# X from strided columns of transposed q, and output rows in token order (linear attention followed by a sentence-level mixture of experts, one core)

## Chip, core and metric

One NeuronCore of a Trainium2 chip runs the kernel; the other cores are idle. The metric is the device time of one execution in microseconds. Three runs of the kernel before took 342.43, 341.39 and 339.92 us, median 341.39.

## What is computed

Eight sentences (batch b) of 576 tokens, eight heads of 64 columns. Linear attention: q gets a softmax over its 64 columns, k a softmax over the tokens, then a 64 x 64 matrix per head is multiplied with q. The result x (576 x 512 for a sentence) goes through one expert of eight, chosen for the whole sentence from the mean of x over its tokens.

```
q_s = softmax(q over d);  k_s = softmax(k over tokens)
kv  = einsum('bhsd,bhse->bhde', k_s, v)
x   = einsum('bhsd,bhde->bhse', q_s, kv)          # then heads side by side: (8, 576, 512)
logits = x.mean(axis=1) @ w_gate;  e = argmax(logits);  gate = softmax(logits)[e]
out[b] = gate * (relu(x[b] @ w1[e]) @ w2[e])      # w1[e]: 512 x 1024, w2[e]: 1024 x 512
```

## The kernel before

**Tokens.** An input tile holds two heads on the 64-partition halves and two in the free dimension; partition p has the nine tokens 9p to 9p + 8 side by side (`pair_src`, L91, with J = 9). So token 9p + j is row p of block j. The transposes of q (L150) are made block by block: column 64j + p of `qt` is token 9p + j. All that follows keeps this blocked order of tokens: x (`xt`), the hidden layer h (`hsb`) and the rows of the output.

**Attention of one sentence** (`attention`, L110) is a generator in steps. Exponentials of q and k on ScalarE (L118, L123), v to fp16 on GpSimd (L129), the sums and the scaling of q on VectorE (L134, L137). For each of two halves i: 18 transposes on TensorE (L150) and two copies to `qt` on VectorE (L157); 18 matmuls k x v (L164); the 128 x 128 `kv` on VectorE (L173). Then for each of two g one chunk c = 2i + g of x: a matmul of 512 columns (L182) and one of 64 (L183), evacuated by VectorE to `xt`, which also adds up the columns for the mean (L184, L188). So a sentence has four chunks. Then the gate's logits (L196), argmax, and the expert's weights by DMAs that GpSimd issues (L211, L216, L217); they are cast from fp32 to fp16 on the way.

**Expert of one sentence** (`moe`, L235 on). Eight blocks of 128 hidden columns: four matmuls of 512 tokens (L243) and four of 64 (L248) each, and a Relu, on ScalarE for even blocks (L253), on VectorE for odd ones (L255); one Relu for all the 64-token tails (L257). Then five output blocks of 128 tokens (64 in the last): eight matmuls (L264), a scaling copy to `osb` on ScalarE (L269), and a store that SyncE issues (L271). `osb` has four buffers. In blocked order rows 128 st to 128 st + 127 are the tokens 9p + 2 st and 9p + 2 st + 1 for all 64 p, so the destination is

```
out_j = out.rearrange("b (p j) d -> b j p d", j=J)        # L96
nc.sync.dma_start(out=out_j[b, js], in_=osb[0:rows])      # L271: 2 x 64 rows of 2 KB, 1 x 64 in the last
```

**Order.** TensorE runs in the order in which the program is written: attention 0 and 1 first; then for each b the steps of the expert of sentence b, with one step of attention b + 2 after each. For sentences 6 and 7 there is no attention beside the expert. The other engines' orders are set by the scheduler of the language; each engine takes its instructions in order. SyncE issues the inputs of six sentences, then the five stores of sentence 0, the inputs of the seventh sentence, the stores of sentence 1, the inputs of the eighth, and then only stores.

Of the kernel before, what the change touches and what calls it, by code (L numbers as in the profile page):

```python
# [19 lines left out]
def kernel(  # L20
# [12 lines left out]
    nc = tc.nc  # L33

    B, H, S, Dh = q.shape
    D, E = moe_w_gate.shape
    F = moe_w1.shape[2]
    J = S // 64
    SM = 512
    ST = S - SM  # L40
    NF = F // 128
    ND = D // 128

# [24 lines left out]
    ones_f32 = consts.tile([128, 1], FP32)  # L68
# [22 lines left out]
    def pair_src(t, b, i):  # L91

        return t[b].rearrange("(i n g) (p j) d -> i (g p) n (j d)", i=2, n=2, p=64)[i]


    out_j = out.rearrange("b (p j) d -> b j p d", j=J)  # L96

    state = {}
    nv = [0]
# [10 lines left out]
    def attention(b, tiles, roomy):  # L110
        xt = xt_pool.tile([128, ND, S], FP16, name="xt")
        pooled = gat_pool.tile([128, ND], FP32, name="pooled")
        x_tag, x_bufs = ("po", 2) if roomy else ("x", 1)
        t_tag = "hm" if roomy else "tk"
        eqs, eks, vas = [], [], []
        for i in range(2):
            eq = e_pool.tile([128, J, 2, Dh], FP16, name="eq")
            nc.scalar.activation(  # L118
                out=eq.rearrange("p j n d -> p n j d"),
                in_=tiles["q", i].rearrange("p n (j d) -> p n j d", j=J), func=AF.Exp,  # L120
            )
            ek = e_pool.tile([128, J, 2, Dh], FP16, name="ek")
            nc.scalar.activation(  # L123
                out=ek.rearrange("p j n d -> p n j d"),
                in_=tiles["k", i].rearrange("p n (j d) -> p n j d", j=J), func=AF.Exp,
            )
            va = v_aug[nv[0] % NVB]
            nv[0] += 1
            nc.gpsimd.tensor_copy(  # L129
                out=va[:, :, 1:].rearrange("p j (n d) -> p n j d", n=2),  # L130
                in_=tiles["v", i].rearrange("p n (j d) -> p n j d", j=J),
            )
            qs = stat.tile([128, J, 2], FP32, name="qs")
            nc.vector.tensor_reduce(out=qs, in_=eq, op=ALU.add, axis=AX.X)  # L134
            qsi = stat.tile([128, J, 2], FP32, name="qsi")
            nc.vector.reciprocal(out=qsi, in_=qs)
            nc.vector.tensor_tensor(  # L137
                out=eq, in0=eq, in1=qsi.unsqueeze(3).to_broadcast([128, J, 2, Dh]), op=ALU.mult,
            )
            eqs.append(eq)  # L140
            eks.append(ek)
            vas.append(va)
        yield
        for i in range(2):
            eq, ek, va = eqs[i], eks[i], vas[i]
            tps = [bank(t_tag, 2) for g in range(2)]
            for j in range(J):
                for g in range(2):
                    r = slice(64 * g, 64 * g + 64)
                    nc.tensor.transpose(  # L150
                        out=tps[g].bitcast(FP16)[:, 64 * j:64 * j + 64],
                        in_=eq[r, j], identity=ident[r, r],
                    )
            qts = []
            for g in range(2):
                qt = qt_pool.tile([128, S], FP16, name="qt")
                nc.vector.tensor_copy(out=qt, in_=tps[g].bitcast(FP16)[:, 0:S])  # L157
                qts.append(qt)
            yield
            kps = [bank("tk", 2) for g in range(2)]  # L160
            for j in range(J):
                for g in range(2):
                    r = slice(64 * g, 64 * g + 64)
                    nc.tensor.matmul(  # L164
                        kps[g][:, 0:129], lhsT=ek[r, j], rhs=va[r, j],
                        start=(j == 0), stop=(j == J - 1),
                    )
            kvs = []
            for g in range(2):
                icv = kv_pool.tile([128, 1], FP32, name="icv")  # L170
                nc.vector.reciprocal(out=icv, in_=kps[g][:, 0:1])
                kv = kv_pool.tile([128, 128], FP16, name="kv")
                nc.vector.scalar_tensor_tensor(  # L173
                    out=kv, in0=kps[g][:, 1:129], scalar=icv, in1=blkmask, op0=ALU.mult, op1=ALU.mult,
                )
                kvs.append(kv)
            yield
            for g in range(2):
                c = 2 * i + g
                px = bank(x_tag, x_bufs)  # L180
                pxt = kps[g][:, 192:256]
                nc.tensor.matmul(px, lhsT=kvs[g], rhs=qts[g][:, 0:SM], start=True, stop=True)  # L182
                nc.tensor.matmul(pxt, lhsT=kvs[g], rhs=qts[g][:, SM:S], start=True, stop=True)  # L183
                nc.vector.tensor_tensor_reduce(  # L184
                    out=xt[:, c, 0:SM], in0=px, in1=ones_f32.to_broadcast([128, SM]),
                    scale=1.0, scalar=0.0, op0=ALU.mult, op1=ALU.add, accum_out=pooled[:, c:c + 1],
                )
                nc.vector.tensor_tensor_reduce(  # L188
                    out=xt[:, c, SM:S], in0=pxt, in1=ones_f32.to_broadcast([128, ST]),
                    scale=1.0, scalar=pooled[:, c:c + 1], op0=ALU.mult, op1=ALU.add,  # L190
                    accum_out=pooled[:, c:c + 1],
                )
                yield
        pg = bank(x_tag, x_bufs)
        for c in range(ND):
            nc.tensor.matmul(  # L196
                pg[0:1, 0:E], lhsT=pooled[:, c:c + 1], rhs=wg_sb[:, c, :],
                start=(c == 0), stop=(c == ND - 1),
            )
        zz = gat_pool.tile([1, E], FP32, name="zz")  # L200
        nc.vector.tensor_copy(out=zz, in_=pg[0:1, 0:E])
        mx8 = gat_pool.tile([1, 8], FP32, name="mx8")
        nc.vector.max(out=mx8, in_=zz)
        eidx = gat_pool.tile([1, 8], U32, name="eidx")
        nc.vector.max_index(out=eidx, in_max=mx8, in_values=zz)
        e_val = nc.values_load(eidx[0:1, 0:1], engines=[ET.Pool], min_val=0, max_val=E - 1)
        w1_sb = w_pool.tile([128, ND, F], FP16, name="w1_sb")
        w1_src = moe_w1[ds(e_val, 1)].rearrange("o (i h g e) f -> i h e (o g) f", i=2, h=2, g=2)
        for i in range(2):
            for h in range(2):  # L210
                nc.gpsimd.dma_start(  # L211
                    out=w1_sb[64 * h:64 * h + 64, 2 * i:2 * i + 2, :], in_=w1_src[i, h]
                )
        w2_sb = w_pool.tile([128, NF, D], FP16, name="w2_sb")
        w2_src = moe_w2[ds(e_val, 1)].rearrange("o (c p) n -> p (o c) n", p=128)
        nc.gpsimd.dma_start(out=w2_sb[:, 0:4], in_=w2_src[:, 0:4])  # L216
        nc.gpsimd.dma_start(out=w2_sb[:, 4:8], in_=w2_src[:, 4:8])  # L217

        nmx = gat_pool.tile([1, 1], FP32, name="nmx")
        nc.vector.tensor_single_scalar(out=nmx, in_=mx8[:, 0:1], scalar=-1.0, op=ALU.mult)  # L220
        ex = gat_pool.tile([1, E], FP32, name="ex")
        sm = gat_pool.tile([1, 1], FP32, name="sm")
        nc.scalar.activation(out=ex, in_=zz, func=AF.Exp, bias=nmx, accum_out=sm)
        gt = gat_pool.tile([1, 1], FP32, name="gt")
        nc.vector.reciprocal(out=gt, in_=sm)  # L225
        state[b] = [xt, gt, w1_sb, w2_sb]
        yield
        pg2 = bank(x_tag, x_bufs)
        nc.tensor.matmul(pg2[:, 0:1], lhsT=ones_row, rhs=gt, start=True, stop=True)
        gate = gat_pool.tile([128, 1], FP32, name="gate")  # L230
        nc.vector.tensor_copy(out=gate, in_=pg2[:, 0:1])
        state[b][1] = gate
        yield

    def moe(b):  # L235
        xt, gate, w1_sb, w2_sb = state.pop(b)
# [23 lines left out]
        for st in range(5):  # L260
            rows = 128 if st < 4 else ST
            po = bank("po", 2)
            for fc in range(NF):
                nc.tensor.matmul(  # L264
                    po[0:rows], lhsT=hsb[:, fc, st * 128:st * 128 + rows], rhs=w2_sb[:, fc, :],
                    start=(fc == 0), stop=(fc == NF - 1),
                )
            osb = o_pool.tile([128, D], FP32, name="osb")
            nc.scalar.mul(osb[0:rows], po[0:rows], gate[0:rows])  # L269
            js = slice(2 * st, min(2 * st + 2, J))  # L270
            nc.sync.dma_start(out=out_j[b, js], in_=osb[0:rows])  # L271
            yield

    def drain(gen):
# [51 lines left out]
```

## Time and profile before

| what | value |
|---|---|
| median of 3 runs | 341.39 us |
| profiled execution | 341.65 us |
| its span (first to last instruction) | 340.0 us |
| mean granted TensorE clock | 0.85 |
| TensorE busy | 193.5 us (57%) |
| VectorE busy | 123.6 us (36%) |
| ScalarE busy | 89.6 us (26%) |
| GpSimd busy | 52.1 us (15%) |
| DMA queue of SyncE (inputs, stores) | 17856 packets, 37.75 MB, 31.4% of 16 engines |
| DMA queue of GpSimd (weights) | 13056 packets, 16.78 MB, 29.3% of 16 engines |

No engine is busy for more than 57% of the span, and the two DMA queues together take 61% of the sixteen DMA engines. Busy time is an average over stages, so it does not say what is waited for; the chain of work that ended last, the waits and the timelines do. DMA share is the mean over the core's 16 DMA engines: one engine working all the time is 1/16 = 0.06. It can come out over 1 where packets overlap on an engine. Stretches are given in us from the start of the span.

### The profile page before, as it was taken

To read this page: it belongs to the slowest core of one execution; us is meant where nothing else is said; L and a number is where in the kernel's file an instruction comes from. 1 tells how busy PE (TensorE), PEld (TensorE's weight loads), DVE (VectorE), ACT (ScalarE), POOL (GpSimd) and SP (SyncE) were. 2 spreads that over 40 slices of the span, in tenths; PEclk is the share of its full clock that TensorE was granted. 3 is DMA by queue.
4 is the path that set the end of the run, shared out by engine and by line. 5 is a ranking of instruction groups with operands and counts; after the bars stand their busy time and mean duration, and the time that the engine had idled before them with its cause. 6 is when DMAs were issued, how large, how long until landed. Compare 5 with 4: busy or idle time off the path is not lost.

```text
span 340.0 us, 4144 instructions
## 1 busy us (share of the span) xinstructions
PE 193.5 (57%) x1552; PEld 95.5 (28%) x1552; DVE 123.6 (36%) x365; ACT 89.6 (26%) x130; POOL 52.1 (15%) x73
## 2 busy tenths in 40 slices
PE   0344387880068930889107895960769885479400
PEld 0223144440024420344103443530335341134100
DVE  3699949510058110780106816710236020011000
ACT  2644235210044300442004434210123230123100
POOL 1325261330001410014100141040000400000000
PEclk9999999995559985699755999996779998599955
DMA  7999999999619791199811149179121781112111
GB/s 262 396 391 378 278 294 280 290 284 285 139 65 332 197 187 36 58 338 223 149 36 64 41 80 196 43 140 166 37 67 52 140 150 38 65 51 66 51 64 42
DMA packets 31508, 54.81 MB, mean 161 GB/s; under 512 B 2304, under 2 KB 10496, under 8 KB 31488
## 3 DMA queue, kind: packets, MB, share of 16 engines
q1 hardware_dynamic: 17856, 37.75, 31.4%
q0 software_dynamic: 13056, 16.78, 29.3%
q8 instruction: 12, 0.20, 0.2%
q10 hardware_dynamic: 576, 0.02, 0.1%
q14 instruction: 8, 0.07, 0.1%
HBM read 61.88 MB, written 9.44 MB: 210 GB/s over the span
## 4 chain that ended last, share of the span: by engine, by line
DMA 48%; DVE 19%; PE 18%; ACT 5%; issue 2%; SPq 1%; ACTq 1%; POOL 0%; DVEq 0%; POOLq 0%
DMA out_dram<-osb 45%; PE hm L243 8%; DVE qs L134 5%; PE po L264 5%; DVE eq L137 4%; DVE xt L184 3%; ACT osb L269 2%; DMA wg_sb<-in_moe_w_gate_dram 2%; DVE hsb L255 2%; ACT eq L118 2%; PE x L182 1%; DMA v_in<-in_v_dram 1%; DVE kv L173 1%; SPq L271 1%; ACT hsb L253 1%
## 5 line engine op out<-in xcount | busy, mean ns | idle before, releaser
L243 PE MATMUL hm<-xt,w_sb 128*128 128x512 f16 x256 | 74.5, 421 | 60.9 <-ACT hsb L253 60.9
L264 PE MATMUL po<-w_sb,hsb 128*128 128x512 f16 (+1 forms) x320 | 77.8, 393 | 22.9 <-ACT osb L269 22.9
L269 ACT ACTIVATE osb<-po,gate 128x512 f32<-128x512 f32 (+1 forms) x40 | 27.2, 686 | 151.6 <-DMA out_dram<-osb 120.8
L264 PEld LDWEIGHTS <-hsb 128*128 128x128 f16 (+1 forms) x320 | 31.0, 103 | 61.0 <-issue 31.3
L243 PEld LDWEIGHTS <-w_sb 128*128 128x128 f16 x256 | 22.5, 105 | 88.0 <-issue 72.6
L134 DVE TENSOR_REDUCE qs<-eq 128x18 f32<-128x1152 f16 x16 | 21.5, 1345 | 64.9 <-ACT eq L118 64.9
L129 POOL CAST va<-v_in 128x1152 f16<-128x1152 f32 x16 | 19.7, 1239 | 132.7 <-PE tk L164 82.2
L255 DVE TENSOR_SCALAR hsb<-hm 128x512 f16<-128x512 f32 x32 | 22.1, 690 | 44.6 <-PE hm L243 44.0
L211 POOL DMA_DIRECT2D w_sb<-in_moe_w_dram x32 | 19.3, 623 | 81.6 <-DVE gt L225 39.6
L253 ACT ACTIVATE hsb<-hm 128x512 f16<-128x512 f32 x32 | 18.8, 588 | 41.8 <-PE hm L243 41.8
L157 DVE COPY qt<-tk 128x576 f16<-128x576 f16 x24 | 9.9, 453 | 52.7 <-PE tk L150 52.7
L248 PEld LDWEIGHTS <-w_sb 128*128 128x128 f16 x256 | 17.7, 104 | 18.1 <-issue 5.4
L137 DVE TENSOR_TENSOR eq<-eq,qsi 128x1152 f16<-128x1152 f16 x16 | 21.8, 1360 | 0.1
L118 ACT ACTIVATE eq<-q_in 128x1152 f16<-128x1152 f32 x16 | 18.6, 1160 | 9.8 <-DMA q_in<-in_q_dram 5.7
L123 ACT ACTIVATE ek<-k_in 128x1152 f16<-128x1152 f32 x16 | 18.5, 1157 | 7.5 <-PE tk L164 4.2
L248 PE MATMUL ht<-xt,w_sb 128*128 128x64 f16 x256 | 19.2, 200 | 0.0
L184 DVE CUSTOM_DVE_ANT_0 xt<-x,ones_f 128x512 f16<-128x512 f32 x24 | 16.4, 684 | 6.6 <-PE tk L183 6.6
L182 PE MATMUL x<-qt,kv 128*128 128x512 f16 x24 | 10.8, 449 | 11.6 <-DVE kv L173 7.0
L164 PE MATMUL tk<-va,ek 64*128 64x129 f16 x288 | 13.8, 246 | 2.9 <-DVE pooled L188 1.9
L164 PEld LDWEIGHTS <-ek 64*128 64x128 f16 x288 | 10.5, 108 | 4.1 <-issue 2.1
L150 PEld LDWEIGHTS <-eq 64*128 64x128 f16 x288 | 6.4, 103 | 12.6 <-issue 11.8
L182 PE MATMUL po<-qt,kv 128*128 128x512 f16 x8 | 4.4, 612 | 9.3 <-DVE kv L173 9.3
(49 smaller groups left out, 106.1 us busy)
## 6 DMA issues: line engine op xcount, KB each, us to landing
q_in<-in_q_dram SPq DMA_DIRECT2D x16, 576.0 KB
k_in<-in_k_dram SPq DMA_DIRECT2D x16, 576.0 KB
v_in<-in_v_dram SPq DMA_DIRECT2D x16, 576.0 KB
w_sb<-in_moe_w_dram POOLq DMA_DIRECT2D x32, 256.0 KB, 10.6
w_sb<-in_moe_w_dram POOLq DMA_DIRECT2D x16, 512.0 KB, 20.7
out_dram<-osb SPq DMA_DIRECT2D x32, 256.0 KB
out_dram<-osb SPq DMA_DIRECT2D x8, 128.0 KB
wg_sb<-in_moe_w_gate_dram ACTq DMA_DIRECT2D x4, 4.0 KB
```

Of the source, the lines that this page charges most:

```text
L118: nc.scalar.activation(out=eq.rearrange("p j n d -> p n j d"), in_=tiles["q", i].rearrange("p n (j d) -> p n j d", j=J), func=AF.Exp,)
L129: nc.gpsimd.tensor_copy(out=va[:, :, 1:].rearrange("p j (n d) -> p n j d", n=2), in_=tiles["v", i].rearrange("p n (j d) -> p n j d", j=J),)
L134: nc.vector.tensor_reduce(out=qs, in_=eq, op=ALU.add, axis=AX.X)
L137: nc.vector.tensor_tensor(out=eq, in0=eq, in1=qsi.unsqueeze(3).to_broadcast([128, J, 2, Dh]), op=ALU.mult,)
L164: nc.tensor.matmul(kps[g][:, 0:129], lhsT=ek[r, j], rhs=va[r, j], start=(j == 0), stop=(j == J - 1),)
L184: nc.vector.tensor_tensor_reduce(out=xt[:, c, 0:SM], in0=px, in1=ones_f32.to_broadcast([128, SM]), scale=1.0, scalar=0.0, op0=ALU.mult, op ...
L243: nc.tensor.matmul(phm, lhsT=w1_sb[:, c, fsl], rhs=xt[:, c, 0:SM], start=(c == 0), stop=(c == ND - 1),)
L248: nc.tensor.matmul(pht[:, fc * ST:(fc + 1) * ST], lhsT=w1_sb[:, c, fsl], rhs=xt[:, c, SM:S], start=(fc == 0 and c == 0), stop=(fc == NF - ...
L253: nc.scalar.activation(out=hsb[:, fc, 0:SM], in_=phm, func=AF.Relu)
L255: nc.vector.tensor_single_scalar(out=hsb[:, fc, 0:SM], in_=phm, scalar=0.0, op=ALU.max)
L264: nc.tensor.matmul(po[0:rows], lhsT=hsb[:, fc, st * 128:st * 128 + rows], rhs=w2_sb[:, fc, :], start=(fc == 0), stop=(fc == NF - 1),)
L269: nc.scalar.mul(osb[0:rows], po[0:rows], gate[0:rows])
```

## The change

The X matmul reads the columns of `qt` in the order of tokens. `qn` is `qt` seen as (p, j): nine columns 64 apart, then the next p. The first matmul takes p from 0 to 55 (56 x 9 = 504 tokens), the second the remaining 8 x 9 = 72; before it was 512 and 64. So `xt`, `hsb` and the output rows are in the natural order of tokens, and rows 128 st to 128 st + 127 of the output are one contiguous block, to which the store writes. The expert's code is otherwise the same, with its 512 and 64 tokens.

```diff
--- before.py
+++ after.py
@@ -38,6 +38,7 @@
     J = S // 64
     SM = 512
     ST = S - SM
+    XM = 56 * J
     NF = F // 128
     ND = D // 128
 
@@ -91,9 +92,6 @@
     def pair_src(t, b, i):
 
         return t[b].rearrange("(i n g) (p j) d -> i (g p) n (j d)", i=2, n=2, p=64)[i]
-
-
-    out_j = out.rearrange("b (p j) d -> b j p d", j=J)
 
     state = {}
     nv = [0]
@@ -178,15 +176,16 @@
             for g in range(2):
                 c = 2 * i + g
                 px = bank(x_tag, x_bufs)
-                pxt = kps[g][:, 192:256]
-                nc.tensor.matmul(px, lhsT=kvs[g], rhs=qts[g][:, 0:SM], start=True, stop=True)
-                nc.tensor.matmul(pxt, lhsT=kvs[g], rhs=qts[g][:, SM:S], start=True, stop=True)
+                pxt = kps[g][:, 192:192 + S - XM]
+                qn = qts[g].rearrange("q (j p) -> q p j", j=J)
+                nc.tensor.matmul(px[:, 0:XM], lhsT=kvs[g], rhs=qn[:, 0:56], start=True, stop=True)
+                nc.tensor.matmul(pxt, lhsT=kvs[g], rhs=qn[:, 56:64], start=True, stop=True)
                 nc.vector.tensor_tensor_reduce(
-                    out=xt[:, c, 0:SM], in0=px, in1=ones_f32.to_broadcast([128, SM]),
+                    out=xt[:, c, 0:XM], in0=px[:, 0:XM], in1=ones_f32.to_broadcast([128, XM]),
                     scale=1.0, scalar=0.0, op0=ALU.mult, op1=ALU.add, accum_out=pooled[:, c:c + 1],
                 )
                 nc.vector.tensor_tensor_reduce(
-                    out=xt[:, c, SM:S], in0=pxt, in1=ones_f32.to_broadcast([128, ST]),
+                    out=xt[:, c, XM:S], in0=pxt, in1=ones_f32.to_broadcast([128, S - XM]),
                     scale=1.0, scalar=pooled[:, c:c + 1], op0=ALU.mult, op1=ALU.add,
                     accum_out=pooled[:, c:c + 1],
                 )
@@ -267,8 +266,7 @@
                 )
             osb = o_pool.tile([128, D], FP32, name="osb")
             nc.scalar.mul(osb[0:rows], po[0:rows], gate[0:rows])
-            js = slice(2 * st, min(2 * st + 2, J))
-            nc.sync.dma_start(out=out_j[b, js], in_=osb[0:rows])
+            nc.sync.dma_start(out=out[b, st * 128:st * 128 + rows, :], in_=osb[0:rows])
             yield
 
     def drain(gen):
```

Every engine has the same instructions in the same order as before; what differs is widths and shapes. On SyncE's queue, at the end of the first six sentences' inputs and the stores of sentence 0, before:

```order
L106 DMA k_in<-in_k_dram 128x2x576
L106 DMA v_in<-in_v_dram 128x2x576
L271 DMA out_dram<-osb 2x64x512 x4
L271 DMA out_dram<-osb 64x512
L106 DMA q_in<-in_q_dram 128x2x576
```

and there with the change (its lines count two less):

```order
L104 DMA k_in<-in_k_dram 128x2x576
L104 DMA v_in<-in_v_dram 128x2x576
L269 DMA out_dram<-osb 128x512 x4
L269 DMA out_dram<-osb 64x512
L104 DMA q_in<-in_q_dram 128x2x576
```

Nothing moved; the four stores of 128 rows have lost the outer dimension of two, and the last one, of 64 rows, is as it was.

## Rows read from the trace of the kernel before

**Rows 1.** The page's part 4, the chain that ended last.

```profile
DMA 48%; DVE 19%; PE 18%; ACT 5%; issue 2%; SPq 1%; ACTq 1%; POOL 0%; DVEq 0%; POOLq 0%
DMA out_dram<-osb 45%; PE hm L243 8%; DVE qs L134 5%; PE po L264 5%; DVE eq L137 4%; DVE xt L184 3%; ACT osb L269 2%; DMA wg_sb<-in_moe_w_gate_dram 2%; DVE hsb L255 2%; ACT eq L118 2%; PE x L182 1%; DMA v_in<-in_v_dram 1%; DVE kv L173 1%; S
```

**Rows 2.** Waits: engine line <- waited for: us in total, times, longest us.

```profile
ACT osb L269 <- DMA out_dram<-osb: 120.8, 14, 23.8
```

**Rows 3.** ScalarE's timeline: start us, us, engine, line, operation, names, shapes [idle before].

```profile
94.37 0.68 ACT L269 ACTIVATE osb<-po,gate 64x512 f32<-64x512 f32 x1 [23.77 <-DMA out_dram<-osb]
...
111.15 0.69 ACT L269 ACTIVATE osb<-po,gate 128x512 f32<-128x512 f32 x1 [2.31 <-DMA v_in<-in_v_dram]
...
117.13 0.69 ACT L269 ACTIVATE osb<-po,gate 128x512 f32<-128x512 f32 x1 [1.04 <-PE po L264]
135.19 0.68 ACT L269 ACTIVATE osb<-po,gate 64x512 f32<-64x512 f32 x1 [17.38 <-DMA out_dram<-osb]
...
178.58 0.68 ACT L269 ACTIVATE osb<-po,gate 64x512 f32<-64x512 f32 x1 [19.94 <-DMA out_dram<-osb]
...
206.27 0.68 ACT L269 ACTIVATE osb<-po,gate 64x512 f32<-64x512 f32 x1 [3.96 <-DMA out_dram<-osb]
...
220.89 0.69 ACT L269 ACTIVATE osb<-po,gate 128x512 f32<-128x512 f32 x1 [1.42 <-PE po L264]
...
247.87 0.68 ACT L269 ACTIVATE osb<-po,gate 64x512 f32<-64x512 f32 x1 [8.42 <-DMA out_dram<-osb]
...
267.00 0.69 ACT L269 ACTIVATE osb<-po,gate 128x512 f32<-128x512 f32 x1 [1.04 <-PE po L264]
271.79 0.68 ACT L269 ACTIVATE osb<-po,gate 64x512 f32<-64x512 f32 x1 [4.10 <-DMA out_dram<-osb]
...
302.10 0.68 ACT L269 ACTIVATE osb<-po,gate 64x512 f32<-64x512 f32 x1 [4.18 <-DMA out_dram<-osb]
...
311.17 0.69 ACT L269 ACTIVATE osb<-po,gate 128x512 f32<-128x512 f32 x1 [1.18 <-PE po L264]
...
323.26 0.68 ACT L269 ACTIVATE osb<-po,gate 64x512 f32<-64x512 f32 x1 [4.18 <-DMA out_dram<-osb]
```

**Rows 4.** The page's part 6, DMA issues: KB each, median us to landing.

```profile
w_sb<-in_moe_w_dram POOLq DMA_DIRECT2D x32, 256.0 KB, 10.6
...
out_dram<-osb SPq DMA_DIRECT2D x32, 256.0 KB
```

**Rows 5.** Stretches: us, busy PE PEld DVE ACT POOL, PEclk, DMA share, GB/s.

```profile
70.00:84.00 14.00, 4.90 (x60) 2.72 (x59) 1.51 (x3) 0.60 (x1) 1.16 (x1) 0.78 1.11 283
86.00:88.00 2.00, 0.00 (x0) 0.00 (x0) 0.00 (x0) 0.00 (x0) 0.00 (x0) 0.50 1.21 236
90.00:92.00 2.00, 0.00 (x0) 0.00 (x0) 0.00 (x0) 0.00 (x0) 0.00 (x0) 0.50 0.21 49
325.00:330.00 5.00, 0.00 (x0) 0.00 (x0) 0.00 (x0) 0.00 (x0) 0.00 (x0) 0.50 0.13 51
331.00:332.00 1.00, 0.00 (x0) 0.00 (x0) 0.00 (x0) 0.00 (x0) 0.00 (x0) 0.50 0.59 139
```

**Rows 6.** Timeline of the DMA queue that SyncE issues.

```profile
70.46 29.38 SPq L271 DMA_DIRECT2D out_dram<-osb  x5
```

**Rows 7.** Chain in order of time: start us, us, what.

```profile
61.77 0.38 PE x L182
62.18 1.73 PE po L264 x8
...
98.50 0.61 PE x L182
```

**Rows 8.** TensorE's timeline after sentence 3's last output block.

```profile
203.31 1.04 PE L243 MATMUL hm<-xt,w_sb 128*128 128x512 f16 x4
```

**Rows 9.** The page's part 5, one group: busy us, mean ns of one.

```profile
L134 DVE TENSOR_REDUCE qs<-eq 128x18 f32<-128x1152 f16 x16 | 21.5, 1345 | 64.9 <-ACT eq L118 64.9
```

## The prediction

> **What bounds the kernel now.** I read the page's chain first, then the list of waits, then the ScalarE timeline, then the DMA engines in short windows. The chain that ended last is 48% DMA, and nearly all of that (45% of 340.0 us, about 153 us) is one group: the stores of osb to the output [rows 1]. In the list of waits the reader sees on whom that falls: ScalarE, at the copy that scales a finished output block into an osb buffer (L269), stood idle 120.8 us in 14 waits for stores, the longest 23.8 us [rows 2]. There are four osb buffers and five output blocks per sentence, so the fifth copy cannot begin before the first store of its own sentence has landed, and ScalarE takes its work in order: the Relu of the next sentence stands behind that copy, TensorE soon behind the Relu. In the ScalarE timeline the fifth copy of a sentence is the 64-row one; it stands at 94.37, 135.19, 178.58, 206.27, 247.87, 271.79, 302.10 and 323.26 us, each time with a wait for a store in its brackets [rows 3]. I call these moments the marks of sentences 0 to 7.
>
> Why is a store late? It is 256 KB [rows 4]. Where only stores are under way, from 325 to 330 us, the DMA share is 0.13 and 51 GB/s move [rows 5]: two of the sixteen DMA engines work and fourteen are idle. At that pace a store takes 256 KB / 51 GB/s = 5.1 us, and the five of a sentence over 20 us. That it is not the row size is seen from 331 to 332, where the last 64-row store falls: it too moves 2 KB rows, but share and rate rise to 0.59 and 139 GB/s [rows 5]. What differs is the shape: a 128-row store goes to a destination of 2 x 64 rows, the 64-row one to a plain list of 64.
>
> [...]
>
> **The change, part by part.** The destination becomes 128 consecutive rows, the plain shape. From the row of 331 to 332 I take it that such a store spreads over all engines: 256 KB in about 1 us, with issue and landing about 2 us, where the fifth copy leaves it 117.13 + 1.73 - 111.15 = 7.7 us [rows 3, 7]. So I count the waits for stores as gone from sentence 1 on. The gain is not the 153 us of the chain: once the store is no longer late, what is late next is the fifth output block on TensorE, eight matmuls of 1.73 us together [rows 7]. The earliest possible mark of a sentence is thus its fourth copy plus 1.73 us, and I rebuild the run from these.
>
> Sentence 0. The DMA engines are full from 70 to 88 us (share 1.11 and 1.21) with inputs and weights, and down to 0.21 from 90 to 92 [rows 5]. The first store is issued at 70.46 behind these inputs [rows 6], in the same queue. More engines do not help before the inputs are through. I put the first mark at 91.5, against 94.37. All that happens earlier is covered by this full stretch.
>
> Sentences 1 to 7, from mark to earliest next mark [rows 3, 7]: sentence 1 takes 117.13 + 1.73 - 94.37 = 24.5; 2 and 3 repeat its pattern, 24.5 each; 4 has its first copy at 220.89 and the same 7.7 to its fifth, so 22.3; 5 takes 267.00 + 1.73 - 247.87 = 20.9; 7, which has no attention beside it, 311.17 + 4 x 1.73 - 302.10 = 16.0, and 6 the same. Together 148.7 us; the real marks are 228.9 apart, so 80 us are waits.
>
> Not all of that comes back. During a wait TensorE started the next sentence's first block: at 203.31, while the copy stood until 206.27 [rows 8, 3]. Without the wait the first Relu comes after that block (1.04 us) and not right after the copy (0.68), a loss of 0.4, and about as much again from the second block's Relu, which VectorE must do first: 0.8 us each for sentences 4, 6 and 7. Sentences 2, 3 and 5 also began with TensorE at 1.2 GHz after the wait (granted 0.50 in such a wait [rows 5]; an X matmul takes 0.61 us right after one, 0.38 on a warm TensorE [rows 7]), which a busy TensorE no longer has: net 0.6 each for 2 and 3, nothing for 5; sentence 1 still follows a wait and stays. Sum 3.6, so 152.3.
>
> The X matmul reads q with neighbouring columns 128 bytes apart; no row of before has such a read. It processes the same 576 columns (504 + 72 for 512 + 64), so a gain is excluded: the lower bound is nothing. For the upper bound I take the nearest slow reader, VectorE's sum over 1152 columns in 1345 ns, 1.17 ns per column [rows 9], against 1.73 us / 8 / 512 = 0.42 on a warm TensorE: 576 x 0.75 = 0.43 us more per chunk, for the four chunks of each of the attentions 3 to 7, 20 x 0.43 = 8.6 us if none is hidden. I take half speed, the nearer row: a chunk then costs 0.61 instead of 0.38 [rows 7], and about two of four lie on the chain (others end while VectorE still scales eq), in the four sentences 2 to 5: 8 x 0.23 = 1.9 us. VectorE's two evacuations of a chunk handle the same 576 columns, so nothing there. The order of instructions is the same on every engine.
>
> End. Now the last copy starts at 323.26 and the span ends at 340.0, 16.7 us later [rows 3], with four slow stores queued. Then: copy 0.68, issue about 0.5, landing of a 64-row store about 1, and closing work: an estimate of 3.8 us.
>
> Sum: 91.5 + 152.3 + 1.9 + 3.8 = 249.5 us of span. The profiled execution took 341.65 for a span of 340.0, 1.65 more, so 251 us. The median of the runs shown, 341.39, differs from that execution by 0.1%.
>
> **Rivals.** (a) The strided read costs the upper bound: 8.6 in place of 1.9, 258 us. For it: no such read exists in the trace. Against it: TensorE has slack in sentences 1 to 3, where VectorE's softmax holds the chain.
> [...]
> (b) The store spreads, but still waits behind weights. Weights land 10.6 us after issue in the median [rows 4], and are issued beside these stores; if a store landed as late, the fifth copy would stand 10.6 - 7.7 = 2.9 us in each of sentences 1 to 5, 15 us: 266 us. Against it: the weights are asked for only after the last X chunk and the gate, when the first output block of the sentence is already on its way.
> (c) The change does not do what it says: the stores stay at 51 GB/s for another reason, such as writing to memory. Then all waits stay, and with 1.9 for the read it is 344 us. The row of 331 to 332 speaks against it.
> (d) Slower than before: the strided read itself becomes the bound, at L182 between kv and the evacuation of x. It decides when the 20 chunks eat the 92 us between 341.65 and 249.3 (my sum without the read): 4.6 us per chunk, 8 ns per column, 19 times the warm rate. At twice that price the time is 341.65 + 92 = 434 us. Nothing in the trace is that slow.
> (e) Better than forecast: the read is free (1.9), the work behind the waits is hidden as now (3.6), and the first store lands at 88 (3.5): 242 us.
>
> **How the numbers follow.** Forecast (250 to 254 and what lies near) 0.62; (a) 0.15; (b) 0.08; (c) 0.03; (d) 0.02; (e) 0.10. The range 242 to 264 holds (e), the forecast and (a), and leaves (b), (c) and (d) out. A measurement of this kernel tells about 1% from no change; all of the forecast, (a), (b) and (e) are faster by far more: 0.95; (c) is within or near 1%, so 0.03 for the same; slower 0.02.
>
> **What would show it.** Right: no wait of the 64-row copy on a store after sentence 0; DMA share well above 0.13 while stores run; marks near 91.5, 116, 142, 167, 191, 212, 229, 246; end within 4 us of the last copy; an X matmul of about 0.6 us on a warm TensorE. Wrong: the share staying at 0.13 (c); waits of 3 us and more at the copy beside weights (b); X chunks above 0.8 us (a). The forecast as a whole fails if the sentences without store waits take another 2 us each, or if inputs and weights turn out to be waited for after 92 us.

## The result and the profile after

The changed kernel takes 257.3 us (median of 4 runs, 256.86 to 258.05) against 340.77 us before (median of 4 runs). The ratio is 0.755 with a 95% interval of 0.751 to 0.758: a quarter of the time is gone. The forecast was 251 us with a range of 242 to 264, so the range held, and so did the account of the stores; the time came out 6 us above the forecast and lies nearest to rival (a), 258 us, which had a chance of 0.15. The profiled execution took 258.05 us for a span of 256.4.

The page's chain that ended last answers to [rows 1]. The reader is to see that the 45% of the stores have become 8%, and that TensorE now holds 65%: with the output blocks, the hidden blocks, and, third, the X matmul (L181) at 9%, which was 1% before.

```profile
PE 65%; DVE 19%; DMA 11%; ACT 2%; issue 1%; ACTq 1%
PE po L263 26%; PE hm L242 20%; PE x L181 9%; DMA out_dram<-osb 8%; DVE qs L132 7%; DVE eq L135 3%; DMA wg_sb<-in_moe_w_gate_dram 2%; PE ht L247 2%; DVE hsb L254 2%; PE tk L148 2%; DVE xt L183 1%; PE po L181 1%; DVE kv L171 1%; PE tk L182 1%; DVE qt L155 1%
```

ScalarE's timeline has the marks again, the fifth copies of sentences 0 to 7 (L268 now; columns as in [rows 3]). Only the first still waits for a store. All others wait 1.16 us for their own output block, as forecast.

```profile
91.02 0.68 ACT L268 ACTIVATE osb<-po,gate 64x512 f32<-64x512 f32 x1 [18.40 <-DMA out_dram<-osb]
...
117.89 0.68 ACT L268 ACTIVATE osb<-po,gate 64x512 f32<-64x512 f32 x1 [1.16 <-PE po L263]
...
143.89 0.68 ACT L268 ACTIVATE osb<-po,gate 64x512 f32<-64x512 f32 x1 [1.16 <-PE po L263]
...
169.89 0.68 ACT L268 ACTIVATE osb<-po,gate 64x512 f32<-64x512 f32 x1 [1.16 <-PE po L263]
...
194.89 0.68 ACT L268 ACTIVATE osb<-po,gate 64x512 f32<-64x512 f32 x1 [1.16 <-PE po L263]
...
218.87 0.68 ACT L268 ACTIVATE osb<-po,gate 64x512 f32<-64x512 f32 x1 [1.16 <-PE po L263]
...
235.56 0.68 ACT L268 ACTIVATE osb<-po,gate 64x512 f32<-64x512 f32 x1 [1.16 <-PE po L263]
...
252.26 0.68 ACT L268 ACTIVATE osb<-po,gate 64x512 f32<-64x512 f32 x1 [1.16 <-PE po L263]
```

The list of waits says the same in one row, where [rows 2] had 14 waits and 120.8 us (us in total, times, longest):

```profile
ACT osb L268 <- DMA out_dram<-osb: 18.4, 1, 18.4
```

The DMA engines in short stretches (columns as in [rows 5]): they are full until 90 us (from 88 on the share was 0.66 before the change). From 246 to 254 only stores are under way, and there the share is 0.35 in the mean, pauses between them included, where it was 0.13 without a pause.

```profile
88.00:90.00 2.00, 0.00 (x0) 0.00 (x0) 0.00 (x0) 0.00 (x0) 0.00 (x0) 0.50 1.15 282
92.00:96.00 4.00, 2.93 (x10) 0.96 (x10) 2.74 (x7) 2.77 (x4) 0.00 (x0) 0.50 0.60 143
120.00:124.00 4.00, 3.32 (x36) 1.66 (x34) 3.85 (x9) 2.14 (x3) 1.17 (x1) 1.00 1.10 261
246.00:254.00 8.00, 6.17 (x29) 2.56 (x26) 0.00 (x0) 2.74 (x4) 0.00 (x0) 1.00 0.35 131
```

The groups of the X matmul (busy us, mean ns of one): 1.008 us for 504 columns and 0.301 for 72. In [rows 7] the 512 columns took 0.61 us right after a wait and 0.38 on a warm TensorE, that is, one with the granted clock at 1.00.

```profile
L181 PE MATMUL x<-qt,kv 128*128 128x504 f16 x24 | 24.2, 1008 | 6.3 <-DVE kv L171 6.3
...
L182 PE MATMUL tk<-qt,kv 128*128 128x72 f16 x32 | 9.6, 301 | 0.0
```

And in the chain in order of time (start us, us, what): the matmul takes 1.01 us at 95.15, where the granted clock is 0.50, and 1.00 us at 122.74, where it is 1.00 (stretches above). It takes the same at either level. Where a block of matmuls stands behind it, as at 182.33, the chain counts 0.85 of it.

```profile
95.15 1.01 PE x L181
...
122.74 1.00 PE x L181
...
182.33 0.85 PE x L181
```

### The profile page after: what moved, and what is told of

Same layout as the page of the kernel before. It is cut to its first block, busy times and chain, and to the rows that moved or that the text cites. A ratio compares the mean times of both kernels' runs of the same rounds, so it can differ in the third digit from the quotient of the medians.

```text
span 256.4 us, 4144 instructions
## 1 busy us (share of the span) xinstructions
PE 202.7 (79%) x1552; PEld 94.3 (37%) x1552; DVE 124.8 (49%) x365; ACT 91.1 (36%) x130; POOL 54.0 (21%) x73
## 4 chain that ended last, share of the span: by engine, by line
PE 65%; DVE 19%; DMA 11%; ACT 2%; issue 1%; ACTq 1%
PE po L263 26%; PE hm L242 20%; PE x L181 9%; DMA out_dram<-osb 8%; DVE qs L132 7%; DVE eq L135 3%; DMA wg_sb<-in_moe_w_gate_dram 2%; PE ht L247 2%; DVE hsb L254 2%; PE tk L148 2%; DVE xt L183 1%; PE po L181 1%; DVE kv L171 1%; PE tk L182 1%; DVE qt L155 1%
## 5 line engine op out<-in xcount | busy, mean ns | idle before, releaser
L242 PE MATMUL hm<-xt,w_sb 128*128 128x512 f16 x256 | 69.9, 400 | 15.3 <-ACT hsb L252 15.3
L263 PE MATMUL po<-w_sb,hsb 128*128 128x512 f16 (+1 forms) x320 | 73.5, 380 | 0.0
L268 ACT ACTIVATE osb<-po,gate 128x512 f32<-128x512 f32 (+1 forms) x40 | 27.5, 686 | 68.3 <-PE po L263 43.6
L242 PEld LDWEIGHTS <-w_sb 128*128 128x128 f16 x256 | 22.6, 102 | 50.1 <-issue 34.0
L127 POOL CAST va<-v_in 128x1152 f16<-128x1152 f32 x16 | 21.5, 1354 | 91.2 <-PE tk L162 40.5
L155 DVE COPY qt<-tk 128x576 f16<-128x576 f16 x24 | 9.9, 453 | 39.8 <-PE tk L148 39.8
L181 PE MATMUL x<-qt,kv 128*128 128x504 f16 x24 | 24.2, 1008 | 6.3 <-DVE kv L171 6.3
L247 PEld LDWEIGHTS <-w_sb 128*128 128x128 f16 x256 | 16.9, 101 | 16.7 <-issue 2.8
L183 DVE CUSTOM_DVE_ANT_0 xt<-x,ones_f 128x504 f16<-128x504 f32 x24 | 16.3, 681 | 6.0 <-PE x L181 5.8
L247 PE MATMUL ht<-xt,w_sb 128*128 128x64 f16 x256 | 18.5, 196 | 0.0
L181 PE MATMUL po<-qt,kv 128*128 128x504 f16 x8 | 7.9, 1018 | 9.4 <-DVE kv L171 9.4
## 6 DMA issues: line engine op xcount, KB each, us to landing
out_dram<-osb SPq DMA_DIRECT2D x8, 128.0 KB, 5.8
```

Source lines behind the costliest of these rows:

```text
L127: nc.gpsimd.tensor_copy(out=va[:, :, 1:].rearrange("p j (n d) -> p n j d", n=2), in_=tiles["v", i].rearrange("p n (j d) -> p n j d", j=J),)
L181: nc.tensor.matmul(px[:, 0:XM], lhsT=kvs[g], rhs=qn[:, 0:56], start=True, stop=True)
L242: nc.tensor.matmul(phm, lhsT=w1_sb[:, c, fsl], rhs=xt[:, c, 0:SM], start=(c == 0), stop=(c == ND - 1),)
L247: nc.tensor.matmul(pht[:, fc * ST:(fc + 1) * ST], lhsT=w1_sb[:, c, fsl], rhs=xt[:, c, SM:S], start=(fc == 0 and c == 0), stop=(fc == NF - ...
L263: nc.tensor.matmul(po[0:rows], lhsT=hsb[:, fc, st * 128:st * 128 + rows], rhs=w2_sb[:, fc, :], start=(fc == 0), stop=(fc == NF - 1),)
```

## Experiments

The first theory: the gain is the spreading of a store over all sixteen DMA engines, and the missing 6 us are the strided read of X. The times are medians; the kernel before, run beside these, took 342.6 us (e1 to e4), 342.8 (e5 to e7), 342.5 (e8 to e10 and e11).

### e1: the store alone

```diff
-            js = slice(2 * st, min(2 * st + 2, J))
-            nc.sync.dma_start(out=out_j[b, js], in_=osb[0:rows])
+            nc.sync.dma_start(out=out[b, st * 128:st * 128 + rows, :], in_=osb[0:rows])
```

> The kernel before with one part of the change alone: a store goes to 128 consecutive rows, and X still reads q contiguously (so tokens are in blocked order and the output rows stand at other tokens' places). Theory (the stores gain by spreading over 16 DMA engines, and the strided read of X takes back some 7 us): 248 to 251 us, X matmul near 0.38 us on a warm TensorE, marks of sentences 1 to 5 some 24.5, 25, 25, 23 and 21 us apart. Rival (the 7 us over the forecast come from the stores or from the sentences themselves, not from the read): 256 to 258 us.

Measured: 249.5 us, ratio 0.729 (0.725 to 0.732), span 248.0. The theory's time holds and the rival falls. That a store spreads over all sixteen engines is not shown by itself, since no view has an engine alone: with stores alone under way the share reaches 0.69 in the changed kernel (250 to 251 us) and 0.92 in e2 (243 to 244). X is back at its old duration, 0.40 us in the mean, and the one wait for a store left is that of sentence 0.

```profile
L182 PE MATMUL x<-qt,kv 128*128 128x512 f16 x24 | 9.6, 401 | 12.8 <-DVE pooled L184 6.5 <-DVE kv L173 6.3
```

```profile
ACT osb L269 <- DMA out_dram<-osb: 20.9, 1, 20.9
```

The marks stand 24.6, 24.9, 24.9, 23.2 and 21.6 us apart for sentences 1 to 5.

### e2: is it the contiguous block?

```diff
-            js = slice(2 * st, min(2 * st + 2, J))
-            nc.sync.dma_start(out=out_j[b, js], in_=osb[0:rows])
+            for h in range(rows // 64):
+                nc.sync.dma_start(out=out_j[b, 2 * st + h], in_=osb[64 * h:64 * h + 64])
```

> The kernel before, blocked order and contiguous X, but each store of 2 x 64 rows issued as two stores of 64 rows. The pieces in memory are just as scattered as before. Theory (the shape decides over how many engines a store is spread): 248 to 252 us, DMA share well above 0.13 while stores run, no wait of the fifth copy after sentence 0. Rival (it is the contiguous 256 KB block that makes the store fast): the stores stay at 51 GB/s and the time at 335 to 345 us.

Measured: 250.5 us, ratio 0.732 (0.729 to 0.735). The rows of an output block lie nine rows apart in memory, as before the change, and the time is about 1 us above e1's. So neither the contiguous block nor the order of tokens is worth anything here; the shape of the transfer is. One of its stretches at the end, with stores alone (columns as in [rows 5]), shows the share, where 2 x 64 rows gave 0.13 (325 to 330 us in [rows 5]):

```profile
245.00:246.00 1.00, 0.00 (x0) 0.00 (x0) 0.00 (x0) 0.15 (x1) 0.00 (x0) 1.00 0.64 141
```

### e3: the strided read alone

```diff
+    out_j = out.rearrange("b (p j) d -> b j p d", j=J)
...
-            nc.sync.dma_start(out=out[b, st * 128:st * 128 + rows, :], in_=osb[0:rows])
+            js = slice(2 * st, min(2 * st + 2, J))
+            nc.sync.dma_start(out=out_j[b, js], in_=osb[0:rows])
```

> The changed kernel with the old store to 2 x 64 rows: strided X alone (tokens are in natural order, and the output rows stand at other tokens' places). Theory (the waits for stores set the pace and cover the read): 339 to 345 us, X matmul 1.0 us as in the changed kernel, stores at 51 GB/s. Rival (the read costs its 0.6 us a chunk whatever stands beside it, 20 chunks and more): 352 to 361 us.

Measured: 345.0 us, ratio 1.0075 (1.0030 to 1.0119): some 2.4 us slower than before, at the upper edge of what the theory said. X takes its 1.0 us, the stores stay at 51 GB/s (share 0.13 from 329 to 334 us), and the waits for stores shrink from 120.8 to 109.6 us: the slow stores cover most of the read.

```profile
ACT osb L270 <- DMA out_dram<-osb: 109.6, 14, 22.2
```

```profile
L183 PE MATMUL x<-qt,kv 128*128 128x504 f16 x24 | 24.2, 1009 | 7.7 <-DVE kv L173 7.7
```

The same read costs 7.8 us in the changed kernel (257.3 against e1's 249.5), where nothing covers it. The two halves of the change do not add up like independent ones.

### e4 and e9: the reordering in VectorE's copy

```diff
-                nc.vector.tensor_copy(out=qt, in_=tps[g].bitcast(FP16)[:, 0:S])
+                tp = tps[g].bitcast(FP16)[:, 0:S]
+                if g == 0:
+                    nc.vector.tensor_copy(
+                        out=qt.rearrange("q (p j) -> q j p", j=J), in_=tp.rearrange("q (j p) -> q j p", j=J)
+                    )
+                else:
+                    nc.vector.tensor_copy(
+                        out=qt.rearrange("q (p j) -> q p j", j=J), in_=tp.rearrange("q (j p) -> q p j", j=J)
+                    )
...
+                nc.tensor.matmul(px[:, 0:XM], lhsT=kvs[g], rhs=qts[g][:, 0:XM], start=True, stop=True)
```

This is e4: for g = 0 the copy writes with a step, for g = 1 it reads with a step. e9 takes the second form for both.

> The changed kernel with the reordering moved from the X matmul to VectorE's copy to qt, so that X reads contiguously; for g = 0 the copy writes with a step of nine columns, for g = 1 it reads PSUM with a step of 64. Theory: X falls back to 0.38 us on a warm TensorE; the copies grow from 0.45 us to 0.6 to 0.9 us, and with VectorE on part of the chain the time is 249 to 253 us. Rival (a strided access on VectorE costs as much as on TensorE, four times): copies of 1.8 us, 256 us and more.

Measured: 270.8 us, a miss for the theory. The groups of the copies (busy us, mean ns) show which form is to blame: writing SBUF with a step of nine columns takes 2.70 us, six times the plain copy's 0.45, while reading PSUM with a step of 64 takes 0.95.

```profile
L157 DVE COPY qt<-tk 128x576 f16<-128x576 f16 x12 | 32.4, 2696 | 38.9 <-PE tk L148 38.9
...
L161 DVE COPY qt<-tk 128x576 f16<-128x576 f16 x12 | 11.4, 950 | 0.0
```

> As e4, with the form of copy that was the cheaper there for all: VectorE reads PSUM with a step of 64 columns and writes qt contiguously (0.95 us a copy against 0.45). X reads contiguously, stores go to 128 consecutive rows. Theory (VectorE is on the chain in part, 0.5 us more for each of four copies a sentence, of which one to two show): 252 to 257 us. Rival (the copies' 2 us a sentence all show, in five sentences and more): 259 to 262 us.

Measured: 252.6 us, ratio 0.738 (0.736 to 0.739), near the lower end of the theory. The reading copy takes 0.75 us here, not the 0.95 it took behind the slow copy in e4; why it was longer there was not looked into.

```profile
L155 DVE COPY qt<-tk 128x576 f16<-128x576 f16 x24 | 17.1, 753 | 38.9 <-PE tk L148 38.9
```

This version has natural order and contiguous stores like the changed kernel and is 4.7 us quicker: a copy takes 0.3 us more and a matmul 0.6 us less. How much of either lies on the chain was not taken apart.

### e5, e6 and e11: what the read costs, and why

Each kernel gives the four chunks of X four orders of reading, on lines of their own. Of the new lines one of each kernel is shown here.

```diff
-                qn = qts[g].rearrange("q (j p) -> q p j", j=J)
...
+                    qn = qts[g].rearrange("q (j p e) -> q p j e", j=J, e=2)
...
+                    qn = qts[g].rearrange("q (x y e) -> q x e y", x=8, e=2)
...
+                    qn = qts[g][:, 1:1 + S].rearrange("q (j p e) -> q p j e", j=J, e=2)
```

The first is chunk 1 of e5, runs of two columns (chunk 0 reads as in the change, chunk 2 runs of four, chunk 3 contiguously). The second is chunk 0 of e6, a step of two columns (4, 8 and 18 in the other chunks). The third is chunk 1 of e11, runs of two from columns stored one column further on (runs of 2, 2, 4, 4 at offsets of 0, 1, 2, 0). Each was run once (249.9, 254.4 and 250.7 us); what is read from them is the duration of the matmuls, six to a group.

> The changed kernel with another order of columns in each chunk of X (so the order of tokens differs from chunk to chunk): chunk 0 single columns 128 bytes apart, chunk 1 runs of two neighbouring columns, chunk 2 runs of four, chunk 3 contiguous. [...] Theory B (each jump costs a fixed time, about 1.2 ns, whatever the run): with 504, 252 and 126 jumps 1.0, 0.7, 0.53 and 0.38 us. Theory C (any non-contiguous pattern takes the slow rate): 1.0 us for chunks 0 to 2.

> The changed kernel with another step between successive columns in each chunk of X (the order of tokens differs from chunk to chunk): steps of 2, 4, 8 and 18 columns, that is 4, 8, 16 and 36 bytes. [...] Theory B (any step other than one is slow): all four 1.0 us. Theory C (it is only long steps, such as the 128 bytes of the change, that are slow): all four near 0.38 us.

e5, the X matmul's groups for chunks 0 to 3 (L182, L186, L190, L194; busy us, mean ns of one): 1.007, 0.590, 0.387 and 0.374 us.

```profile
L182 PE MATMUL x<-qt,kv 128*128 128x504 f16 x6 | 6.0, 1007 | 3.2 <-DVE kv L171 3.2
L186 PE MATMUL x<-qt,kv 128*128 128x504 f16 x6 | 3.5, 590 | 0.0
...
L190 PE MATMUL x<-qt,kv 128*128 128x504 f16 x6 | 2.3, 387 | 2.7 <-DVE kv L171 2.7
...
L194 PE MATMUL x<-qt,kv 128*128 128x504 f16 x6 | 2.2, 374 | 3.7 <-DVE pooled L196 3.7
```

e6, for steps of 4, 8, 16 and 36 bytes (L182, L186, L190, L194): 0.430, 0.611, 1.060 and 1.026 us. The 0.430 is a mean over two clocks: one of the six, at 94.88 us in a stretch granted 0.50, took 0.60, and the median is 0.398 (ns, lowest, median and highest):

```profile
L190 PE MATMUL x<-qt,kv 128*128 128x504 f16 x6 | 6.4, 1060 | 2.7 <-DVE kv L171 2.7
L194 PE MATMUL x<-qt,kv 128*128 128x504 f16 x6 | 6.2, 1026 | 0.0
L186 PE MATMUL x<-qt,kv 128*128 128x504 f16 x6 | 3.7, 611 | 2.8 <-DVE pooled L196 2.8
...
L182 PE MATMUL x<-qt,kv 128*128 128x504 f16 x6 | 2.6, 430 | 3.2 <-DVE kv L171 3.2
```

```profile
L182 PE MATMUL x<-qt,kv x6: 388/398/602, 52.5 to 196.1; 128*128 128x504 f16 x6
```

In e5 B and C miss runs of two and of four (0.59 and 0.39 measured; B had 0.7 and 0.53, C 1.0 for both). In e6 B misses two steps and C three. What fits is another count: how often the read goes to another group of eight neighbouring columns, 16 bytes, counted from the first column of a tile (e11 calls a group a line). The size is read from e6: with groups of 8 bytes the step of 8 bytes would have 504 visits like the step of 16 and take as long (0.611 against 1.060 measured), and with groups of 32 bytes the step of 16 bytes would have 277 and, by the price below, take some 0.63 us. The count is an estimate from the measured times. The contiguous matmul is 504 columns at 0.42 ns, 210 ns, and 164 more for everything else. Taking these 164 off, chunk 0 of e5 is 843 ns for 504 visits, 1.67 ns each; runs of two 426 ns for 252 visits, 1.69 each; a step of 8 bytes 447 ns for the same 252, 1.77; runs of four have 126 visits, 210 ns by that price, just what the columns take, and so should be (nearly) free: 0.387 us against 0.374. This count was made after the fact, so it got a run of its own.

> As e5 (the order of tokens differs from chunk to chunk), with q's columns stored at an offset in each chunk, so that runs of neighbouring columns do or don't cross the borders of 16-byte lines: chunk 0 runs of two, offset 0 (no run crosses); chunk 1 runs of two, offset 1 (one run in four crosses); chunk 2 runs of four, offset 2 (every second run crosses); chunk 3 runs of four, offset 0 (none crosses). Theory (each visit of a 16-byte line takes 1.67 ns, which hides 4 columns at 0.42 ns): 252, 315, 189 and 126 visits, matmuls of 0.59, 0.69, 0.48 and 0.39 us on a warm TensorE. Rival (it is the jump between runs that costs, wherever the lines lie): 0.59, 0.59, 0.39 and 0.39 us.

```profile
L187 PE MATMUL x<-qt,kv 128*128 128x504 f16 x6 | 4.2, 695 | 2.4 <-DVE pooled L197 2.4
L183 PE MATMUL x<-qt,kv 128*128 128x504 f16 x6 | 3.5, 590 | 3.6 <-DVE kv L172 3.6
L191 PE MATMUL x<-qt,kv 128*128 128x504 f16 x6 | 2.9, 490 | 2.7 <-DVE kv L172 2.7
...
L195 PE MATMUL x<-qt,kv 128*128 128x504 f16 x6 | 2.3, 377 | 2.4 <-DVE pooled L197 2.4
```

Measured for chunks 0 to 3 (L183, L187, L191, L195): 0.590, 0.695, 0.490 and 0.377 us; the theory said 0.59, 0.69, 0.48 and 0.39. The runs are the same in chunks 0 and 1 and in 2 and 3; only where they lie against the groups differs. So the times go with the visits, and the jump theory falls. (The step of 4 bytes in e6, 126 visits, fits too: 0.40 on a warm TensorE. The step of 16 bytes, 504 visits, stays some 0.05 us above the count, 1.060 against 1.007; that is open.)

### e7: buffers instead of engines

```diff
-    o_pool = ctx.enter_context(tc.tile_pool(name="o", bufs=4))
+    o_pool = ctx.enter_context(tc.tile_pool(name="o", bufs=8))
```

> The kernel before with eight osb buffers instead of four, nothing else. Theory (two DMA engines carry 32 stores of 5.1 us, 163 us, beside their sixteenth of inputs and weights, 61% less the stores' own share, so they are busy nearly all the time and set the pace): waits for stores move to other copies, 325 to 340 us. Rival (the pace is set by the fifth copy's wait for one of four buffers, and more buffers hide the slow stores): 255 to 280 us.

Measured: 334.0 us, ratio 0.974 (0.967 to 0.981). Waiting for stores falls from 120.8 to 69.7 us, and the time by 2.6% only:

```profile
ACT osb L269 <- DMA out_dram<-osb: 69.7, 12, 12.1
```

The first mark comes at 71.75 us, 22.6 earlier than before, but the later stores lag: after the last mark the span goes on for 32.5 us (331.6 - 299.1), with nothing but stores under way.

```profile
299.11 0.68 ACT L269 ACTIVATE osb<-po,gate 64x512 f32<-64x512 f32 x1 [4.33 <-DMA out_dram<-osb]
```

A sum suggests why: if two DMA engines are behind a store, as a share of 0.13 is read here, they have as much work as the span is long. From the page of before: 61% of sixteen engines' 340 us is 206 us per engine in the mean, of which the stores are 163 x 2 / 16 = 20; so each engine has about 186 us of inputs and weights, and the two have 163 us of stores on top, 349 us, about the span. That sum is worked out from the page, not measured per engine, it supposes that all stores share the same two, and it comes out somewhat high, as shares do that go over 1 (1.11 and 1.21 in [rows 5]); that buffers hardly help, and that stores are left over at the end, is measured.

### e8: the last wait

```diff
-    o_pool = ctx.enter_context(tc.tile_pool(name="o", bufs=4))
+    o_pool = ctx.enter_context(tc.tile_pool(name="o", bufs=8))
...
+            for h in range(rows // 64):
+                nc.sync.dma_start(out=out_j[b, 2 * st + h], in_=osb[64 * h:64 * h + 64])
```

> The stores as two of 64 rows each (blocked order, contiguous X, as in e2) and eight osb buffers instead of four. In e2 one wait for a store is left, 20.9 us at the fifth copy of sentence 0, since its first store stands behind the inputs in the same queue. Theory (that wait is a matter of buffers, and TensorE is the bound behind it): the wait goes, the first mark comes at 72 us, and the time falls by 12 to 20 us to 231 to 239 us. Rival (the DMA engines are full until 90 us, and what the next sentence needs lands no sooner, so the wait only moves to inputs or weights): 246 to 251 us.

Measured: 230.8 us, ratio 0.674 (0.672 to 0.676), at the lower edge of the theory and the quickest of all, 10% under the changed kernel. The first mark comes at 71.44, and what is left of the waits for stores is one of 1.2 us.

```profile
71.44 0.68 ACT L269 ACTIVATE osb<-po,gate 64x512 f32<-64x512 f32 x1 [1.16 <-PE po L264]
...
96.40 0.68 ACT L269 ACTIVATE osb<-po,gate 64x512 f32<-64x512 f32 x1 [1.16 <-PE po L264]
```

```profile
ACT osb L269 <- DMA out_dram<-osb: 1.2, 1, 1.2
```

The eight buffers that gave 9 us with stores of 2 x 64 rows (e7) give 20 here (250.5 to 230.8): with quick stores they only have to bridge the one stretch in which the queue is full of inputs.

### e10: does the outer size set the number of engines?

```diff
-    out_j = out.rearrange("b (p j) d -> b j p d", j=J)
+    out_j = out.rearrange("b (p j) d -> b j p d", j=2 * J)
...
-            js = slice(2 * st, min(2 * st + 2, J))
+            js = slice(4 * st, min(4 * st + 4, 2 * J))
```

> The kernel before with the destination of a store cut as 4 x 32 rows instead of 2 x 64 (and 2 x 32 for the last, 64-row one; the output rows stand at other tokens' places); nothing else. Theory (the outermost dimension of the destination sets the number of DMA engines): four engines, DMA share 0.25 and about 100 GB/s where 128-row stores run alone, a store in 2.6 us, waits for stores a small part of those before, 252 to 275 us. Rival (any scattered destination, whatever its outer size, runs at 51 GB/s): 335 to 345 us. Other rival (what matters is that a store is not one plain list; the number of engines is not the outer size): a share that is neither 0.13 nor 0.25.

Measured: 292.2 us, ratio 0.853 (0.851 to 0.855). The share is as the theory says: where stores run alone at the end, 0.26 and 102 GB/s (columns as in [rows 5]), twice what 2 x 64 rows gave (0.13 and 51) and about 4/16. That these are four engines is read from the share; no view shows the engines singly.

```profile
282.00:284.00 2.00, 0.00 (x0) 0.00 (x0) 0.00 (x0) 0.00 (x0) 0.00 (x0) 1.00 0.26 102
```

The time is a miss: 65.8 us are still waited for stores, in 10 waits, where I expected a small part.

```profile
ACT osb L269 <- DMA out_dram<-osb: 65.8, 10, 22.7
```

The longest of them, 22.7 us, is that of sentence 0, which e1 has too (20.9). The other nine, 43.1 us, are new against e1; half of that is one wait before the mark of sentence 2:

```profile
164.22 0.68 ACT L269 ACTIVATE osb<-po,gate 64x512 f32<-64x512 f32 x1 [21.36 <-DMA out_dram<-osb]
```

During it the DMA share is 1.08 and 1.14 (140 to 150 us) and 0.89 (150 to 155), and then 0.29 and 0.28 until the wait ends: for the last 9 us the share is the 0.26 of stores alone and little more. So the stores, at 2.6 us each when alone, fell behind while the engines were full of inputs and weights, and had to be caught up at that share; how the other waits split was not measured.

## Why the forecast was right, and where it was off

The steps of the forecast beside the changed kernel and beside e1, which is the changed kernel's store without its read (us; a sentence's time goes from mark to mark):

| step | forecast | changed kernel | e1 |
|---|---|---|---|
| first mark | 91.5 | 91.0 | 91.3 |
| sentence 1 | 24.5 | 26.9 | 24.6 |
| sentences 2 and 3, each | 25.6 | 26.0 | 24.9 |
| sentence 4 | 23.6 | 25.0 | 23.2 |
| sentence 5 | 21.4 | 24.0 | 21.6 |
| sentences 6 and 7, each | 16.8 | 16.7 | 16.7 |
| end after the last mark | 3.8 | 4.1 | 4.2 |
| span | 249.5 | 256.4 | 248.0 |

**Why a store was late.** Right, and shown by the shares with stores alone: 0.13 for 2 x 64 rows, 0.26 for 4 x 32 (e10), 0.69 in one us for plain rows (changed kernel, 250 to 251) and 0.64 for two plain halves (e2); as engines that is two, four and many, an estimate from the shares. I put issue and landing of a plain 128-row store at about 2 us; the page of the changed kernel has 4.2 in the median (KB each, us to landing), which the 7.7 us before the fifth copy still cover. Of the 3.8 us of the end no row gives the 0.5 of the issue or the closing work apart; measured is the whole, 4.1 us.

```profile
out_dram<-osb SPq DMA_DIRECT2D x32, 256.0 KB, 4.2
```

Rival (c), a store that is slow for another reason, has fallen with e2.

**The gain is less than the chain's share.** Right: the chain had 153 us on the stores; the time fell by 83, and by 93 in e1. Rebuilding the sentences from their earliest marks gave 247.6 us of span without any cost of the read (249.5 - 1.9); e1, which has none, has 248.0.

**The first mark.** Right: it is set mainly by the inputs in front of the first store; the store's own speed moved it from 94.37 to 91.0 only. That it need not be waited for at all (e8) I had not seen.

**The work hidden under the waits.** I gave 3.6 us in all. In e1 sentences 2 to 7 together differ from that part of the sum, without the read, by less than half a microsecond (128.0 against 127.8). The 1.2 GHz that the forecast gives TensorE after a wait is in the traces a granted share of 0.50: before the change from 135.2 to 138.0 us, 178.6 to 182.0 and 248.5 to 250.0, in sentences 2, 3 and 5. As a rate, four matmuls of 512 columns take 1.71 us on the chain of the changed kernel at 0.50 (96.28) and 0.86 at 1.00 (123.87), that is 1.2 and 2.4 columns per ns.

**The read of X.** This is the step that failed, in the words of the prediction: "I take half speed, the nearer row: a chunk then costs 0.61 instead of 0.38". That the read may cost something was seen; how much was not. A read at half speed would be 0.84 ns per column (twice 0.42), my upper bound was 1.17, and measured are 1.67, a quarter of the warm rate. So the upper bound was none: a slow reader on another engine set no limit to this one. The X matmul of 1.0 us is also over the 0.8 that I had named as the sign of rival (a). At a granted clock of 0.50 the read takes the same 1.0 us (95.15), where a contiguous one takes 0.61 (98.50 in [rows 7]). So sentence 1, two of whose chunks run in a stretch granted 0.50 and to which I gave no cost, lost 2.3 us as well. Per chunk the read costs 576 x (1.67 - 0.42) = 0.72 us more, for 20 chunks 14.4; the table shows 8.7 (2.3 + 1.1 + 1.1 + 1.8 + 2.4), so 60% of it is on the chain, twelve chunks' worth, where I had counted eight. In 2 and 3 VectorE covers more: in e1 the second X matmul of a pair still waits 0.73 us for VectorE's evacuation (122.85), in the changed kernel it has no wait there (124.86). In 4, from its second half on, and in 5 TensorE itself is the chain. Rival (a) with its 258 us came out in time, by two errors that cancel: a price too low, and all of it counted as visible. That is luck. Had none of the 14.4 us been hidden, the time would have been some 264 us by this sum (247.6 + 14.4 + 1.65), the edge of the range.

**Weights in the way of stores** (rival b): no. After sentence 0 no fifth copy waits for a store. **The read as the bound** (rival d): no; 1.67 ns per column is far from the 8 it would have taken.

## What to carry to other kernels

Where transfers ran alone at a share near a small multiple of 1/16, the multiple was in both cases here the outermost dimension of the transfer (0.13 for 2 x 64 rows, 0.26 for 4 x 32): look at that dimension of its shape before its size, its rows or its buffers, and make it the long one (64 or 128 rows here, with shares of 0.64 and 0.69), if need be by cutting the transfer in two. Do that on the DMA's side: moving the order of the data into a matmul's read cost 7 us here that two stores of 64 rows did not (257.3 against 250.5). And when a wait goes, rebuild the time from what is late next; the chain's share of the waits was nearly twice the gain.

## What the runs showed of the hardware

The strided matmuls of e5, e6 and e11 that are slower than the contiguous one take, beside the 164 ns, 1.67 to 1.78 ns for each visit of a group of eight fp16 columns, 16 bytes; that is an estimate from their times. On a warm TensorE, for 504 columns, four columns per visit take 0.38 to 0.40 us (contiguous 0.37), two 0.59 to 0.61 and one 1.01 to 1.06; three were not tried. At a granted clock of 0.50 runs of two cost nothing: right after the wait of sentence 0 in e5, the matmul with runs of two (L186) takes 0.61 us, as contiguous columns do there in [rows 7], and single columns (L182) 1.01. These are e5's stretch (columns as in [rows 5]) and TensorE's timeline in it:

```profile
92.00:98.00 6.00, 5.16 (x21) 1.96 (x20) 4.63 (x11) 2.06 (x3) 0.00 (x0) 0.50 0.85 273
```

```profile
94.44 1.01 PE L182 MATMUL x<-qt,kv 128*128 128x504 f16 x1 [0.84 <-DVE kv L171]
...
97.30 0.61 PE L186 MATMUL x<-qt,kv 128*128 128x504 f16 x1
```

VectorE's copy of 576 fp16 columns from PSUM takes 0.45 us plain (L155 of the changed kernel), 0.75 us with a step of 64 columns on the reading side (e9), and 2.70 us with a step of nine columns, 18 bytes, on the writing side (e4).
